# Small routing and choice work from GpSimd to VectorE, the last two diagonals to ScalarE, scatters and zero stores a step sooner, and row loads ahead of weight loads, in a recurrence, mixture and feed-forward kernel

## The chip, the cores and the metric

The kernel runs on one core of a Trainium2 chip. The metric is the device time of one execution in microseconds (us). TensorE (PE) multiplies matrices and writes PSUM; VectorE (DVE), ScalarE (ACT) and GpSimd (POOL) work element by element; SyncE (SP) issues most DMA transfers, GpSimd the indirect ones (scatters). Each engine carries out its own instructions in order, and waits at an instruction until what it needs is there.

## The reference

The computation has three parts. A recurrence over 768 time steps (batch 4, 8 heads, head size 48) gives 3072 rows of 384 numbers; a mixture of eight experts sends each row to the expert with the largest logit; a feed-forward part follows.

```python
for t in range(S):                       # S = 768, per batch and head
    cur = einsum('bhd,bhe->bhde', u[None] * kt, vt)
    y[:, :, t] = einsum('bhd,bhde->bhe', rt, state + cur)
    state = w[None, :, :, None] * state + einsum('bhd,bhe->bhde', kt, vt)
...
logits = x @ w_gate                      # x: 3072 x 384, 8 experts
expert_idx = argmax(logits, axis=1)
for e in range(E):
    h = maximum(xe @ w1[e], 0.0)         # 384 -> 1024
    out[mask] = gate_w[mask, None] * (h @ w2[e])   # 1024 -> 384
...
h = x @ w_in                             # 384 -> 2048
return maximum(0.01 * h, h) @ w_out      # 2048 -> 384
```

For the reference's inputs the eight experts get 410, 409, 403, 389, 380, 374, 359 and 348 rows.

## The kernel before

**Attention.** The recurrence is done in chunks: 24 units (`n`, 6 chunks of 128 tokens times 4 batches), and a loop of 25 steps that is software-pipelined by hand. In step `n` PE makes the scores of unit `n` (L490), the values of unit `n-1` (L520, L526), its state update (L511, for units under 20) and turns the values of unit `n-2` into rows (L565). DVE lays the masked scores over the diagonal (L496), scales K and R of unit `n+2` (L432) and sums `av` (L460). POOL makes `kr` (L451, for units under 20) and `rk` (L446, L447) of unit `n+3`. ACT writes the diagonal `A` of unit `n+1` as eight activations (L479); for units 22 and 23 POOL writes it as one product (L472). SP loads inputs ahead and, from step `ZERO_AT`, stores zeros over the spare rows of one expert region per step (L415).

**Routing.** Four units are a group. `ROUTE_AT` puts the four parts of a group's routing at fixed steps: part 0 the largest logit (L707 to L716), part 1 the one-hot choice `oh` (L718 to L726), part 2 the prefix counts on PE and the running count `carry` (L732 to L748), part 3 the row index `ix` (L751 to L755). On steps under 20 POOL does a part of it. `SCATTER_AT` puts the scatters (L759, issued by POOL) of each unit's 128 rows into the DRAM table `xs`, one region per expert. `choose_first` (steps 16 to 18) picks the expert that leads after three groups, and `early_flag` (steps 20, 21) tells whether that one has 256 rows after four.

**Experts.** The leading expert starts early, with a window of its first 256 rows, loaded by POOL as soon as the scatters of groups 0 to 3 have landed (L864, step 21); its other 224 follow as window 1, after all scatters. Windows 2 to 8 are the other experts, by size, with a fixed room each (`CAPS`). A window's rows are loaded as `w` partitions times `nj` rows (L861 to L866) into the one buffer `erows`, turned on PE (L880), split into two fp32r parts `xe` (ACT L883, DVE L884), and multiplied in eight steps (`first` L903, `second` L928). Beside it come the weights: one piece of 384 KB per step (L781, three `raw` buffers), of which ACT rounds the high part (L794) and DVE or POOL takes the low part (L802), and the conversion of 64-bit weights (load L812, ACT L822, DVE L832 to L852, store L854). The last part (L1022, L1041) is 414 us of PE work.

The order on each engine is the order of the code: nothing is reordered by a scheduler. On SP the row load of the next window stands behind the weight piece of the same step:

```python
if n + AHEAD >= nf:
    self.piece_load(n + AHEAD)
if n >= nf:
    if f == 0 and i + 1 < len(WINDOWS):
        self.load_rows(i + 1, xs)
```

Of the kernel before, what the change touches and what calls it, by code (L numbers as in the profile page):

```python
# [21 lines left out]
P = 128  # L22
NC = S // P
NU = NC * B
# [9 lines left out]

TB = 4

WARM = 5
ZERO_AT = 3

VO = 5  # L40

SCATTER_AT = {
    **{11 + 4 * g + u: [(g, u)] for g in (0, 1) for u in range(4)},
    19: [(2, 0), (2, 1)],
    20: [(2, 2), (2, 3)],
    21: [(3, u) for u in range(4)],
    24: [(4, u) for u in range(4)],
}

# [14 lines left out]
LISTS = 4  # L64
OUT_AT = (0, 1, 3, 5, 7, 9, 11, 13)

CAPS = (480, 456, 432, 416, 400, 392, 384, 372)
EARLY = 256
WINDOWS = [(0, 0, EARLY), (0, EARLY, CAPS[0] - EARLY)] + [(k, 0, CAPS[k]) for k in range(1, 8)]
PAD = 260  # L70
# [14 lines left out]
class Kernel:  # L85
# [149 lines left out]

    def choose_first(self, keep, part):

        V, G = self.nc.vector, self.nc.gpsimd
        if part == 0:
            f = lambda nm, w=1, dt=F32: keep.tile([1, w], dt, name=nm)  # L240
            _, self.half_key = self.counts(keep, "half", G)
            self.half_mx, self.half_x, self.half_id = f("half_mx"), f("half_x", E), f("half_id")
            self.lead, self.first_i = f("lead", E), f("first_i", 1, I32)
        elif part == 1:
            V.tensor_reduce(out=self.half_mx, in_=self.half_key, axis=AX.X, op=ALU.max)
            G.tensor_scalar(
                out=self.lead, in0=self.half_key, scalar1=self.half_mx, scalar2=None, op0=ALU.is_equal
            )
            G.tensor_tensor(out=self.half_x, in0=self.lead, in1=self.place, op=ALU.mult)
        else:  # L250
            V.tensor_reduce(out=self.half_id, in_=self.half_x, axis=AX.X, op=ALU.add)
            G.tensor_scalar(
                out=self.first_i, in0=self.half_id, scalar1=float(E - 1), scalar2=0.0, op0=ALU.min, op1=ALU.max
            )

# [8 lines left out]

    def early_flag(self, keep, part):

        V, G = self.nc.vector, self.nc.gpsimd
        if part == 0:
            self.early_cnt, _ = self.counts(keep, "early", G)
            G.tensor_tensor(out=self.early_cnt, in0=self.early_cnt, in1=self.lead, op=ALU.mult)  # L270
        else:
            self.redo = n = keep.tile([1, 1], F32, name="early_n")
            V.tensor_reduce(out=n, in_=self.early_cnt, axis=AX.X, op=ALU.add)
            V.tensor_scalar(out=n, in0=n, scalar1=float(EARLY), scalar2=None, op0=ALU.is_lt)
# [70 lines left out]
    def attention(self, xs, clist, extra, first_weights, const, route):  # L345
        nc, tc, a = self.nc, self.tc, self.a
        with ExitStack() as ctx:
# [27 lines left out]
            nc.sync.dma_start(out=u1, in_=a["u"])  # L375
            self.u_row = one.tile([P, DM], F32, name="u_row")
            load(0, ("k", "r", "kT", "rT"))
            load(1, ("kT", "rT", "k", "r"))
            load(0, ("v",))
            load(2, ("k", "r"))  # L380
            load(1, ("v",))
# [82 lines left out]
            def prep_diag(n):  # L464
                if n >= NU:
                    return
                d = st[n]
                d["A"] = wk.tile([P, 2, NP, P], F32, tag="A", name="A")
                if n >= NU - 2:

                    flat = d["A"].rearrange("s i p t -> s p i t")
                    nc.gpsimd.tensor_tensor(  # L472
                        out=flat, in0=self.ident[:, None, None, :].to_broadcast([P, NP, 2, P]),
                        in1=d["av"].rearrange("s (p i) -> s p i", i=2)[:, :, :, None].to_broadcast([P, NP, 2, P]),
                        op=ALU.mult,
                    )
                    return
                for h in range(H):
                    nc.scalar.activation(  # L479
                        out=d["A"][:, h % 2, h // 2, :], in_=self.ident, func=AF.Copy,  # L480
                        scale=d["av"][:, h : h + 1],
                    )
# [113 lines left out]
            for n in range(NU + 1):  # L596

                ahead = [n + 2] if n < 18 else [2 * n - 16, 2 * n - 15] if n < 20 else []
                for m in ahead:
                    load(m, ("kT", "rT"))  # L600
                for m in ahead:
                    load(m + 1, ("k", "r"))
                if n == 19:

                    first_weights()
                for m in ahead:
                    load(m, ("v",))
# [12 lines left out]
                if 0 <= n - 1 < NU:  # L620
                    values(n - 1)
                    update(n - 1)
                if 0 <= n - 2 < NU - 1:
                    rows(n - 2)

                rows_out(n - 3)
                if n - 2 >= B:
                    state(n - 2)

                if n < NU:  # L630
                    masked(n)
                if 0 < n <= B:
                    state(n - 1)
                prep_T(n + 2)
                if n:
                    prep_kr2(n + 1)
                prep_rk(n + 3)
                if 0 < n <= VO:
                    values_out(n - 1)
                if n + 1 < NU - 2:  # L640
                    prep_diag(n + 1)
                prep_av(n + 2)
                if n + 2 >= NU - 2:
                    prep_diag(n + 2)
                if VO <= n - 1 < NU:
                    values_out(n - 1)
                decay(n - 1)
                extra(n)
                if n == 3:
                    self.late_tables(one, route, const)  # L650
                elif n == 5:
                    self.later_tables(one, const)
                elif n == NU - 2:
                    self.safe_decays(one, const)
                    self.cap_table()
                for part, g in ROUTE_AT.get(n, ()):
                    bank = None
                    if part == 2:
                        bank = st[n - 1].get("bank") or update_bank(n - 1)
                        bank = bank[:, NP * D : NP * D + 5 * E]  # L660

                    self.route(part, g, route, nc.gpsimd if n < 20 else nc.vector, bank)
                if 16 <= n < 19:
                    self.choose_first(const, n - 16)
                elif 20 <= n < 22:
                    self.early_flag(const, n - 20)
                for g, u in SCATTER_AT.get(n, ()):
                    self.scatter(g, u, xs)
                if n == NU - 3:

                    self.load_rows(0, xs, nc.gpsimd)
# [24 lines left out]
    def route(self, part, g, sm, eng, bank=None):  # L696
# [20 lines left out]
        elif part == 1:  # L717
            nc.scalar.activation(out=d["ex"][:, :, 0:E], in_=d["df"], func=AF.Exp)  # L718
            d["m2"], d["oh"] = f("m2", [P, B]), f("oh16", [P, B, E], BF16)
            V.tensor_reduce(out=d["m2"], in_=d["eq"], axis=AX.X, op=ALU.max)  # L720
            if eng is V:
                V.tensor_tensor(out=d["oh"], in0=d["eq"], in1=be(d["m2"]), op=ALU.is_equal)
            else:
                eng.tensor_tensor(out=d["eq"], in0=d["eq"], in1=be(d["m2"]), op=ALU.subtract)
                eng.tensor_scalar(out=d["oh"], in0=d["eq"], scalar1=0.0, scalar2=None, op0=ALU.is_equal)
            eng.tensor_copy(  # L726
                out=d["rows"].bitcast(I32)[:, :, DM + 1], in_=self.tokid[:, B * g : B * (g + 1)]
            )
# [126 lines left out]
            del self.conv[i]  # L855


    def load_rows(self, i, xs, eng=None):

        k, off, cap = WINDOWS[i]  # L860
        nj = -(-cap // P)  # L861
        w = cap // nj
        self.win[i] = t = self.rowpool.tile([P, 4, RW], F32, tag="rows", name="erows")
        (eng or self.nc.sync).dma_start(  # L864
            out=t[:w, :nj, :],
            in_=xs[bass.ds(self.ids[k] * NT + off, cap), :].rearrange("(j p) c -> p j c", p=w),  # L866
        )

    def turn(self, i, ps, tag, cs=range(KD)):
        nc = self.nc  # L870
        k, off, cap = WINDOWS[i]
        nj = -(-cap // P)
        w = cap // nj
        for c in cs:
            if c == 0:
                self.xT[i] = self.xpool.tile([P, 2, KD, 512], F32R, tag="x", name="xe")
# [69 lines left out]
    def experts(self, xs, clist, pools, meanwhile):  # L946
# [10 lines left out]
                self.second(*next(rest), pools)  # L957

        for n, (i, f) in enumerate(seq):
            if n + AHEAD >= nf:  # L960
                self.piece_load(n + AHEAD)
            if n >= nf:
                if f == 0 and i + 1 < len(WINDOWS):
                    self.load_rows(i + 1, xs)
                if f == 6:
                    for k in {1: (1,), 2: (2, 3), 3: (4, 5), 4: (6, 7)}.get(i, ()):
# [341 lines left out]
def main_path(k, ctx, const, out, xs, clist, debug):  # L1308
# [8 lines left out]
            k.piece_load(i)  # L1317

    def extra(n):
        for i in {20: (0,), 21: (1,), 22: (2,), 23: (3, 4), 24: (5,)}.get(n, ()):  # L1320
            k.piece_high(i)
        for i in {21: (0,), 22: (1, 2), 23: (3, 4), 24: (5,)}.get(n, ()):
            k.piece_low(i)
        for i in {21: (3,), 22: (4, 5), 23: (6, 7)}.get(n, ()):
            k.piece_load(i)

    kw = dict(reuse_waits="tile")
# [92 lines left out]
```

## Time and profile before

| | us |
|---|---|
| median of 3 runs | 796.58 (795.02 to 797.38) |
| the profiled execution | 795.89 |
| its span | 794.2 |
| busy in the span: PE, DVE, ACT, POOL | 755.1, 471.9, 372.5, 198.3 |

The span is what the trace holds; 1.69 us of the profiled execution lie around it. All times of the rows count from the start of the span. [...]

### The profile page before, as it was taken

What the parts mean: (1) busy time and instruction counts of PE and PEld (TensorE: products, weight loads), DVE (VectorE), ACT (ScalarE), POOL (GpSimd) and SP (SyncE); (2) the same over time, 40 slices, a digit from 0 to 9 for tenths busy, and PEclk for the clock granted to TensorE, in tenths of its full rate; (3) what the DMA queues carried; (4) which work ended last, traced back from release to release, by engine and by line L of the source; (5) the groups of instructions that cost most, each with busy time, mean ns of one, the idle gap of its engine ahead of it and who ended that gap; (6) DMA issues with size and microseconds to landing.
All of it is one profiled execution on the core that took longest, in us unless ns stands there. A gap on an engine that the chain in (4) does not pass through costs nothing.

```text
span 794.2 us, 13196 instructions
## 1 busy us (share of the span) xinstructions
PE 755.1 (95%) x4908; PEld 694.2 (87%) x4908; DVE 471.9 (59%) x837; ACT 372.5 (47%) x785; POOL 198.3 (25%) x216
## 2 busy tenths in 40 slices
PE   6999995989999999799999999999999999999994
PEld 3889884989999999799999899999999999999993
DVE  6898885548888999699873443433333343343330
ACT  6898873355545555356443523332342243233331
POOL 6867885401222222122200110020020001002001
PEclk9999997899999999999999999999999999999997
DMA  8997965368767757757530000010010001001001
GB/s 250 264 272 225 281 223 179 121 184 257 210 193 230 232 183 232 204 162 228 147 111 21 6 35 1 1 40 0 1 40 1 1 0 40 1 1 40 1 1 44
DMA packets 52372, 92.62 MB, mean 117 GB/s; under 512 B 12788, under 2 KB 30761, under 8 KB 52297
## 3 DMA queue, kind: packets, MB, share of 16 engines
q1 hardware_dynamic: 49017, 81.47, 34.6%
q0 software_dynamic: 3280, 10.21, 3.5%
q8 instruction: 40, 0.66, 0.4%
q14 instruction: 35, 0.29, 0.1%
HBM read 73.11 MB, written 18.57 MB: 115 GB/s over the span
## 4 chain that ended last, share of the span: by engine, by line
PE 75%; DMA 9%; POOL 7%; issue 3%; DVE 2%; SPq 2%; ACT 0%; POOLq 0%; ACTq 0%
PE o L1041 25%; PE ph L1022 25%; PE ph L903 12%; PE y L928 11%; DMA r<-in_r 3%; DMA erows<-xs 3%; DMA xs<-z 2%; POOL rk L446 2%; POOL xs L759 2%; POOL rk L447 1%; PE pt L880 1%; DMA raw<-in_wE 1%; SPq L368 1%; POOL kr L451 1%; DMA xs<-rows,ix 1%
## 5 line engine op out<-in xcount | busy, mean ns | idle before, releaser
L1041 PE MATMUL o<-c,gg 128*128 128x384 f32 x1152 | 215.5, 336 | 0.0
L1022 PE MATMUL ph<-x,c 128*128 128x512 f32 x864 | 213.9, 392 | 0.0
L1041 PEld LDWEIGHTS o<-c,gg 128*128 128x128 f32 x1152 | 202.1, 188 | 8.1 <-DVE gg L1031 0.2
L1022 PEld LDWEIGHTS ph<-x,c 128*128 128x128 f32 x864 | 161.2, 188 | 28.5
L1028 DVE TENSOR_TENSOR s<-s,ph 128x512 f32<-128x512 f32 x96 | 65.9, 686 | 165.4 <-ACT s L1027 165.4
L1027 ACT ACTIVATE s<-ph 128x512 f32<-128x512 f32 x96 | 57.4, 598 | 173.9 <-PE ph L1022 162.7
L903 PE MATMUL ph<-xe,c 128*128 128x256 f32 (+8 forms) x648 | 124.8, 338 | 0.0
L928 PE MATMUL y<-hh,c 128*128 128x256 f32 (+8 forms) x648 | 122.4, 333 | 1.2 <-DVE hh L909 0.7
L802 POOL TENSOR_TENSOR c<-raw,c 128x768 fp32r<-128x768 f32 x32 | 60.2, 1880 | 223.3 <-ACT c L794 159.7
L928 PEld LDWEIGHTS y<-hh,c 128*128 128x128 f32 x648 | 110.2, 189 | 3.7 <-DVE hh L909 0.9
L903 PEld LDWEIGHTS ph<-xe,c 128*128 128x128 f32 x648 | 109.8, 192 | 1.9
L1031 DVE TENSOR_TENSOR gg<-s,gg 128x512 fp32r<-128x512 f32 x96 | 66.4, 692 | 67.0 <-ACT gg L1030 66.3
L1054 POOL DMA_INDIRECT out<-z,to x24 | 24.2, 1008 | 320.9 <-ACT z L1053 302.6
L1030 ACT ACTIVATE gg<-s 128x512 fp32r<-128x512 f32 x96 | 60.7, 632 | 81.2 <-DVE s L1028 81.2
L794 ACT ACTIVATE c<-raw 128x768 fp32r<-128x768 f32 x80 | 67.1, 840 | 6.7 <-DMA raw<-in_wE 5.9
L908 ACT ACTIVATE hh<-ph 128x256 fp32r<-128x256 f32 (+8 forms) x72 | 34.4, 478 | 68.5 <-PE ph L903 65.4
L802 DVE TENSOR_TENSOR c<-raw,c 128x768 fp32r<-128x768 f32 x48 | 46.0, 962 | 13.7 <-ACT c L794 12.0
L479 ACT ACTIVATE A<-ident,av 128x128 f32<-128x128 f32 x176 | 53.8, 396 | 0.5 <-DVE av L460 0.4
L849 DVE SCALAR_TENSOR_TENSOR t<-raw,t 128x384 f32<-128x384 uint32 x32 | 44.3, 1384 | 1.1
L909 DVE SCALAR_TENSOR_TENSOR hh<-ph,hh 128x256 fp32r<-128x256 f32 (+8 forms) x72 | 38.5, 535 | 6.1 <-ACT hh L908 5.9
L496 DVE COPY_PREDICATED A<-strict,pa 128x1024 f32<-128x1024 int32 x24 | 32.4, 1351 | 3.1 <-ACT A L479 1.2
L490 PE MATMUL pa<-R,K 48*128 48x128 f32 x384 | 28.2, 287 | 5.8 <-DVE A L496 5.8
(176 smaller groups left out, 681.1 us busy)
## 6 DMA issues: line engine op xcount, KB each, us to landing
raw<-in_wE SPq DMA_DIRECT2D x64, 384.0 KB
raw<-in_w2nd SPq DMA_DIRECT2D x32, 384.0 KB
w2f<-t SPq DMA_DIRECT2D x32, 192.0 KB
raw<-w2f SPq DMA_DIRECT2D x16, 384.0 KB
k<-in_k SPq DMA_DIRECT2D x24, 192.0 KB
r<-in_r SPq DMA_DIRECT2D x24, 192.0 KB
v<-in_v SPq DMA_DIRECT2D x24, 192.0 KB
kT<-in_kT SPq DMA_DIRECT2D x40, 96.0 KB
```

Source lines behind the costliest of these rows:

```text
L479: nc.scalar.activation(out=d["A"][:, h % 2, h // 2, :], in_=self.ident, func=AF.Copy, scale=d["av"][:, h : h + 1],)
L794: self.nc.scalar.activation(out=w[:, 0, c], in_=t, func=AF.Copy)
L802: eng.tensor_tensor(out=w[:, 1, c], in0=t, in1=w[:, 0, c].bitcast(F32), op=ALU.subtract)
L849: nc.vector.scalar_tensor_tensor(out=x, in0=low.bitcast(U32), scalar=2.0**-52, in1=x, op0=ALU.mult, op1=ALU.mult)
L903: nc.tensor.matmul(ph[:, :cap], w[:, wl, c * 512 + o : c * 512 + o + P], self.xT[i][:, xl, c, :cap], start=(c == 0 and n == 0), stop=(c == ...
L928: nc.tensor.matmul(self.y[i][m][:, :cap], w[:, wl, o : o + P], t[:, xl, :cap], start=(f == 0 and n == 0), stop=(f == FF // P - 1 and n == 2),)
L1022: nc.tensor.matmul(ph, w[:, wl, c * 512 + off : c * 512 + off + P], x2[b][:, xl, c, :], start=(c == 0 and i == 0), stop=(c == KD - 1 and i ...
L1027: nc.scalar.activation(out=s, in_=ph, func=AF.Copy, scale=0.01)
L1028: nc.vector.tensor_tensor(out=s, in0=s, in1=ph, op=ALU.max)
L1030: nc.scalar.activation(out=t[:, 0, :], in_=s, func=AF.Copy)
L1031: nc.vector.tensor_tensor(out=t[:, 1, :], in0=s, in1=t[:, 0, :].bitcast(F32), op=ALU.subtract)
L1041: nc.tensor.matmul(o[b][k][:, :DM], t[:, gl, k * P : (k + 1) * P], w[:, wl, (f % 4) * DM : (f % 4 + 1) * DM], start=(f == 0 and i == 0), s ...
```

## The change

The GpSimd half of part 1 of the routing goes to VectorE in every group, group 3's routing wholly, and `choose_first` and `early_flag` too. The diagonals of units 22 and 23 are written by ScalarE like the others. Scatters, zero stores and the empty list `no_tokens` come a step sooner; the first conversions of weights come a step later. Two warm-up matmuls are left out, and of unit 1 `k` and `r` are loaded before their turned forms. From window 2 on, the row load of the next window stands ahead of the weight piece. The rooms become multiples of 16 (456, 392 and 372 become 448, 400 and 368), and `window` takes the smallest `nj` that divides the room.

```diff
-WARM = 5
-ZERO_AT = 3
+WARM = 3
+ZERO_AT = 2
 SCATTER_AT = {
-    **{11 + 4 * g + u: [(g, u)] for g in (0, 1) for u in range(4)},
...
+    **{10 + 4 * g + u: [(g, u)] for g in (0, 1) for u in range(4)},
...
+    20: [(2, 3), (3, 0)],
+    21: [(3, u) for u in range(1, 4)],
...
-CAPS = (480, 456, 432, 416, 400, 392, 384, 372)
+CAPS = (480, 448, 432, 416, 400, 400, 384, 368)
...
-            _, self.half_key = self.counts(keep, "half", G)
+            _, self.half_key = self.counts(keep, "half")
...
-            G.tensor_tensor(out=self.half_x, in0=self.lead, in1=self.place, op=ALU.mult)
+            V.tensor_tensor(out=self.half_x, in0=self.lead, in1=self.place, op=ALU.mult)
...
-            self.early_cnt, _ = self.counts(keep, "early", G)
+            self.early_cnt, _ = self.counts(keep, "early")
...
-            load(1, ("kT", "rT", "k", "r"))
+            load(1, ("k", "r", "kT", "rT"))
...
-                if n >= NU - 2:
-
-                    flat = d["A"].rearrange("s i p t -> s p i t")
-                    nc.gpsimd.tensor_tensor(
...
-                if n + 1 < NU - 2:
-                    prep_diag(n + 1)
+                prep_diag(n + 1)
                 prep_av(n + 2)
-                if n + 2 >= NU - 2:
-                    prep_diag(n + 2)
...
-                    self.route(part, g, route, nc.gpsimd if n < 20 else nc.vector, bank)
+                    self.route(part, g, route, nc.gpsimd if n < 18 else nc.vector, bank)
...
-            if eng is V:
-                V.tensor_tensor(out=d["oh"], in0=d["eq"], in1=be(d["m2"]), op=ALU.is_equal)
-            else:
-                eng.tensor_tensor(out=d["eq"], in0=d["eq"], in1=be(d["m2"]), op=ALU.subtract)
-                eng.tensor_scalar(out=d["oh"], in0=d["eq"], scalar1=0.0, scalar2=None, op0=ALU.is_equal)
+            V.tensor_tensor(out=d["oh"], in0=d["eq"], in1=be(d["m2"]), op=ALU.is_equal)
...
+    def window(self, i):
+
+        k, off, cap = WINDOWS[i]
+        nj = next(n for n in range(-(-cap // P), 5) if cap % n == 0)
+        return k, off, cap, nj, cap // nj
...
         for n, (i, f) in enumerate(seq):
+
+            if i > 1 and f == 0 and i + 1 < len(WINDOWS):
+                self.load_rows(i + 1, xs)
             if n + AHEAD >= nf:
                 self.piece_load(n + AHEAD)
             if n >= nf:
-                if f == 0 and i + 1 < len(WINDOWS):
+                if i == 1 and f == 0:
                     self.load_rows(i + 1, xs)
...
-        for i in {20: (0,), 21: (1,), 22: (2,), 23: (3, 4), 24: (5,)}.get(n, ()):
+        for i in {21: (0,), 22: (1,), 23: (2, 3, 4), 24: (5,)}.get(n, ()):
             k.piece_high(i)
-        for i in {21: (0,), 22: (1, 2), 23: (3, 4), 24: (5,)}.get(n, ()):
+        for i in {22: (0, 1), 23: (2, 3, 4), 24: (5,)}.get(n, ()):
             k.piece_low(i)
-        for i in {21: (3,), 22: (4, 5), 23: (6, 7)}.get(n, ()):
+        for i in {22: (3, 4), 23: (5, 6, 7)}.get(n, ()):
             k.piece_load(i)
```

On POOL, in steps 19 to 21 of attention, before: `rk` is the product of step 19 and 20, `A` the diagonals, `early_*` the early flag, `DMA xs` the scatters, the last row the load of the first window.

```order
L446 TENSOR_TENSOR rk<-r,k 128x384
L447 TENSOR_TENSOR rk<-rk,u_row 128x384
L724 TENSOR_TENSOR eq<-eq,m_1890 128x32
L725 TENSOR_SCALAR oh_1891<-eq 128x32
...
L472 TENSOR_TENSOR A<-ident,av 128x4x2x128
L230 TENSOR_TENSOR early_cnt<-carry,region 1x8
...
L759 DMA xs<-rows,ix 24576x386 x2
L472 TENSOR_TENSOR A<-ident,av 128x4x2x128
L759 DMA xs<-rows,ix 24576x386 x4
L864 ISA
L864 DMA erows<-xs 128x2x386
```

The same place of the changed kernel (its line numbers are others):

```order
L448 TENSOR_TENSOR rk<-r,k 128x384
L449 TENSOR_TENSOR rk<-rk,u_row 128x384
L745 DMA xs<-rows,ix 24576x386 x2
L448 TENSOR_TENSOR rk<-r,k 128x384
L449 TENSOR_TENSOR rk<-rk,u_row 128x384
L745 DMA xs<-rows,ix 24576x386 x5
L854 ISA
L854 DMA erows<-xs 128x2x386
```

Only the products, the scatters and the load are left there; seven scatters stand in these steps instead of eight.

On ACT, the last steps of attention before: `rows` and `xT` are the outputs of the units, `c` the high parts of the weights, `xe` the turned rows of the first window.

```order
L535 ACTIVATE xT_145<-py 112x512
L545 ACTIVATE St_143<-St_143,pw 112x112 x4
L794 ACTIVATE c_1968<-raw 128x768
L577 ACTIVATE rows<-pr 128x384
L535 ACTIVATE xT_146<-py 112x512
...
L535 ACTIVATE xT_146<-py 112x512
L794 ACTIVATE c_2152<-raw 128x768
L883 ACTIVATE xe<-pt 128x256 x3
```

And of the changed kernel:

```order
L528 ACTIVATE xT_145<-py 112x512
L538 ACTIVATE St_143<-St_143,pw 112x112 x4
L570 ACTIVATE rows<-pr 128x384
L472 ACTIVATE A<-ident,av 128x128 x8
L528 ACTIVATE xT_146<-py 112x512
...
L528 ACTIVATE xT_146<-py 112x512
L780 ACTIVATE c_2156<-raw 128x768
L871 ACTIVATE xe<-pt 128x256 x3
```

The diagonal's eight activations stand in steps 21 and 22, the conversions start a step later, and the piece that precedes `xe` is still the sixth.

On SP, the load of the last window before (`raw<-in_wE` is a weight piece, `raw_4307` the 64-bit weights):

```order
L781 DMA raw<-in_wE 128x768
L781 ISA
L781 DMA raw<-in_wE 128x768
L864 ISA
L864 DMA erows<-xs 124x3x386
L812 DMA raw_4307<-in_w2nd 128x768
```

And of the changed kernel:

```order
L767 DMA raw<-in_wE 128x768
L854 ISA
L854 DMA erows<-xs 92x4x386
L767 ISA
L767 DMA raw<-in_wE 128x768
L798 DMA raw_4314<-in_w2nd 128x768
```

The row load stands one piece further ahead, and its shape is 92 partitions of four rows instead of 124 of three.

## Rows read from the trace of the kernel before

**Rows 1.** PE, end of attention: start, us, what, idle before it.
```profile
90.87 0.18 PE L732 MATMUL pu<-oh,tri 128*128 128x32 bf16 x1 [1.56 <-POOL oh L725]
...
139.53 1.54 PE L880 MATMUL pt<-ident,erows 128*128 128x128 f32 x6 [7.86 <-DMA erows<-xs]
...
142.43 2.85 PE L903 MATMUL ph<-xe,c 128*128 128x256 f32 x18
```

**Rows 2.** The chain that ended last: start, us, what.
```profile
130.17 5.16 DMA xs<-rows,ix
...
164.75 7.23 DMA raw<-in_wE
```

**Rows 3.** Stretches: us, busy PE, PEld, DVE, ACT, POOL, clock, DMA share, GB/s.
```profile
84.60:111.80 27.20, 25.25 (x338) 22.88 (x336) 22.10 (x48) 24.35 (x79) 23.53 (x39) 0.94 0.86 260
111.80:131.60 19.80, 17.84 (x189) 15.35 (x185) 15.97 (x41) 7.24 (x14) 17.30 (x16) 0.91 0.55 189
...
295.00:321.90 26.90, 26.90 (x156) 26.78 (x155) 26.06 (x40) 14.59 (x27) 7.39 (x5) 1.00 0.70 228
```

**Rows 4.** PE, windows 7 and 8.
```profile
318.33 0.49 PE L880 MATMUL pt<-ident,erows 128*128 128x128 f32 x3
...
336.72 0.88 PE L880 MATMUL pt<-ident,erows 124*128 124x124 f32 x3 [5.14 <-DMA erows<-xs]
337.26 3.23 PE L903 MATMUL ph<-xe,c 128*128 128x384 f32 x9
340.29 2.26 PE L928 MATMUL y<-hh,c 128*128 128x384 f32 x9
342.39 1.72 PE L903 MATMUL ph<-xe,c 128*128 128x384 f32 x9
```

**Rows 5.** SP's queue, windows 7 and 8.
```profile
317.67 4.77 SPq L781 DMA_DIRECT2D raw<-in_wE  x2
322.67 0.28 SPq L864 DMA_DIRECT2D erows<-xs  x1
```

**Rows 6.** POOL in order of time, steps 15 and 20 to 21 of attention.
```profile
90.20 0.23 POOL L724 TENSOR_TENSOR eq<-eq,m 128x32 f32<-128x32 f32 x1
...
90.77 0.18 POOL L726 COPY rows<-tokid 128x4 int32<-128x4 int32 x1
...
118.25 0.92 POOL L230 TENSOR_TENSOR early_cnt<-carry,region 1x8 f32<-1x8 f32 x1
...
120.31 1.06 POOL L759 DMA_INDIRECT xs<-rows,ix  x1 [0.38 <-issue]
121.68 2.52 POOL L759 DMA_INDIRECT xs<-rows,ix  x1 [0.30 <-DVE A L496]
124.22 1.91 POOL L472 TENSOR_TENSOR A<-ident,av 128x1024 f32<-128x1024 f32 x1
```

**Rows 7.** ACT, end of attention.
```profile
107.92 2.44 ACT L479 ACTIVATE A<-ident,av 128x128 f32<-128x128 f32 x8
...
132.20 0.84 ACT L794 ACTIVATE c<-raw 128x768 fp32r<-128x768 f32 x1
```

**Rows 8.** One us of the stretch after the last row load's wait.
```profile
338.00:339.00 1.00, 1.00 (x4) 1.00 (x4) 0.76 (x3) 0.89 (x3) 0.00 (x0) 0.50 0.26 101
```

**Rows 9.** ACT, window 7: a piece converted, and the wait behind it.
```profile
328.85 0.84 ACT L794 ACTIVATE c<-raw 128x768 fp32r<-128x768 f32 x1
337.59 0.55 ACT L822 ACTIVATE size<-raw 128x384 f32<-128x384 f32 x1 [7.89 <-DMA raw<-in_w2nd]
```

**Rows 10.** Matmul groups by shape: busy us, mean ns.
```profile
L928 PE MATMUL y<-hh,c 128*128 128x456 f32 x72 | 16.1, 368 | 0.0
...
L928 PE MATMUL y<-hh,c 128*128 128x372 f32 x72 | 13.3, 332 | 0.0
```

**Rows 11.** ACT near the start.
```profile
13.26 0.23 ACT L595 ACTIVATE idwg<-wg 112x32 f32<-112x32 f32 x1 [2.01 <-DMA wg<-in_wg]
```

**Rows 12.** POOL near the start, while zeros are stored.
```profile
42.40 1.01 POOL L446 TENSOR_TENSOR rk<-r,k 128x384 f32<-128x384 f32 x1 [2.06 <-DMA r<-in_r]
```

More of the change, by code (lines that the diff above doesn't have):

```diff
@@ L35 @@
 TB = 4
-WARM = 5
-ZERO_AT = 3
+WARM = 3
+ZERO_AT = 2
 VO = 5
 SCATTER_AT = {
-    **{11 + 4 * g + u: [(g, u)] for g in (0, 1) for u in range(4)},
-    19: [(2, 0), (2, 1)],
-    20: [(2, 2), (2, 3)],
-    21: [(3, u) for u in range(4)],
+    **{10 + 4 * g + u: [(g, u)] for g in (0, 1) for u in range(4)},
+    18: [(2, 0)],
+    19: [(2, 1), (2, 2)],
+    20: [(2, 3), (3, 0)],
+    21: [(3, u) for u in range(1, 4)],
     24: [(4, u) for u in range(4)],
@@ L236, in choose_first @@
     def choose_first(self, keep, part):
-        V, G = self.nc.vector, self.nc.gpsimd
+        V = self.nc.vector
         if part == 0:
             f = lambda nm, w=1, dt=F32: keep.tile([1, w], dt, name=nm)
-            _, self.half_key = self.counts(keep, "half", G)
+            _, self.half_key = self.counts(keep, "half")
             self.half_mx, self.half_x, self.half_id = f("half_mx"), f("half_x", E), f("half_id")
@@ L245, in choose_first @@
             V.tensor_reduce(out=self.half_mx, in_=self.half_key, axis=AX.X, op=ALU.max)
-            G.tensor_scalar(
+            V.tensor_scalar(
                 out=self.lead, in0=self.half_key, scalar1=self.half_mx, scalar2=None, op0=ALU.is_equal
             )
-            G.tensor_tensor(out=self.half_x, in0=self.lead, in1=self.place, op=ALU.mult)
+            V.tensor_tensor(out=self.half_x, in0=self.lead, in1=self.place, op=ALU.mult)
         else:
             V.tensor_reduce(out=self.half_id, in_=self.half_x, axis=AX.X, op=ALU.add)
-            G.tensor_scalar(
+            V.tensor_scalar(
                 out=self.first_i, in0=self.half_id, scalar1=float(E - 1), scalar2=0.0, op0=ALU.min, op1=ALU.max
@@ L265, in early_flag @@
     def early_flag(self, keep, part):
-        V, G = self.nc.vector, self.nc.gpsimd
+        V = self.nc.vector
         if part == 0:
-            self.early_cnt, _ = self.counts(keep, "early", G)
-            G.tensor_tensor(out=self.early_cnt, in0=self.early_cnt, in1=self.lead, op=ALU.mult)
+            self.early_cnt, _ = self.counts(keep, "early")
+            V.tensor_tensor(out=self.early_cnt, in0=self.early_cnt, in1=self.lead, op=ALU.mult)
         else:
@@ L468, in prep_diag @@
                 d["A"] = wk.tile([P, 2, NP, P], F32, tag="A", name="A")
-                if n >= NU - 2:
-                    flat = d["A"].rearrange("s i p t -> s p i t")
-                    nc.gpsimd.tensor_tensor(
[L473 to L477, printed above, removed]
                 for h in range(H):
@@ L855, in convert @@
             del self.conv[i]
+    def window(self, i):
+        k, off, cap = WINDOWS[i]
+        nj = next(n for n in range(-(-cap // P), 5) if cap % n == 0)
+        return k, off, cap, nj, cap // nj
     def load_rows(self, i, xs, eng=None):
-        k, off, cap = WINDOWS[i]
-        nj = -(-cap // P)
-        w = cap // nj
+        k, off, cap, nj, w = self.window(i)
         self.win[i] = t = self.rowpool.tile([P, 4, RW], F32, tag="rows", name="erows")
@@ L870, in turn @@
         nc = self.nc
-        k, off, cap = WINDOWS[i]
-        nj = -(-cap // P)
-        w = cap // nj
+        k, off, cap, nj, w = self.window(i)
         for c in cs:
```

## The prediction

> **What bounds the kernel now.** I read four views in this order. First PE in order of time, with the idle time before each instruction, since PE is busy for 755 of 794 us: what can be won is what PE waits for, or does slowly. In the end of attention PE waits 1.56 us for the one-hot choice that POOL makes, and 7.86 us for the first window's rows, which it turns at 139.53; the first expert matmuls start at 142.43 [rows 1]. Then the chain that ended last: its step before those rows is a scatter issued at 130.17 that takes 5.16 us [rows 2]. From that scatter's start to PE's turn it is 139.53 − 130.17 = 9.36 us, so the first window hangs on when POOL issues its last early scatter. Third the stretches: between 84.6 and 131.6 PE idles 27.20 − 25.25 + 19.80 − 17.84 = 3.9 us, and the clock's means of 0.94 and 0.91 cost about 0.06 × 27.2 + 0.09 × 19.8 = 3.4 us, while POOL is busy for 23.53 of 27.2 and 17.30 of 19.8 us [rows 3]. In the windows later PE has no idle time (26.90 of 26.90), with one exception: the last window's rows come 5.14 us late, and the clock that is at half behind that wait makes the next step slow [rows 4]. SP says why they come late: the row load stands behind two weight pieces, the second of which waits for a buffer, and is issued at 322.67 only [rows 5].
>
> **Routing, choice and diagonals (the start of the first window).** POOL stops doing the following from step 15 on. Fourteen small products and copies of the choice in steps 15 to 19; two instructions there lie 90.77 − 90.20 = 0.57 us apart, so 0.285 us each, 4.0 us. Two diagonals at 1.91 us, 3.8 us. The early flag, from 118.25 to the scatter at 120.31, 2.1 us. One scatter that now stands before these steps: 121.68 − 120.31 = 1.4 us. Together 11.3 us [rows 6]. The scatter at 121.68 took 2.52 us and the one before it 1.06 [rows 6]; if that excess of 1.5 us goes too, it is 12.8. POOL was the late one over this whole stretch [rows 3], so the last early scatter comes at about 130.17 − 11.3 = 118.9, and with the same 9.36 us behind it the rows are there at 128.2. PE itself ends attention at 131.6 now and gets back at most 3.9 + 3.4 = 7.3 us: 124.3, which is sooner than the rows, so a wait of some 4 us stays and it is still the rows that are late.
>
> The moved work lands on engines that have less room than POOL. ACT takes two diagonals of 2.44 us [rows 7] and is at 24.35 of 27.2 us in the first of the stretches, 15.97 of 19.8 us for DVE in the second, and only 7.24 of 19.8 us for ACT there [rows 3], which is where the diagonals go. Conversions of weights, one of them at 132.20 [rows 7], stand ahead of `xe` on ACT and a step later than before. That one, the sixth, comes just behind PE's end of attention at 131.6; with PE's 7.3 us back it would be at 124.9, and as its load now starts a step later, I put it up to 2 us later, at 127: close under the rows' 128.2 but not over. I take −11.0: POOL's 11.3 less a little for these. Bounds: −13 (with the scatter's excess), and −4 where PE's own pace, held by ACT, DVE and a DMA share that is 0.86 at 260 GB/s already [rows 3], is what remains.
>
> **Row loads ahead of weight pieces.** Before, the last row load was issued at 322.67 and its rows were used at 336.72, 14.0 us later [rows 4, 5]. Now it waits only for its buffer, which PE's last turn of window 7 frees at 318.33 + 0.49 = 318.8 [rows 4]; with 0.28 us for the issue, 319.1, that is 3.6 us sooner. 368 rows are 1% fewer bytes than 372, so by the nearest row it takes 14.0 us again and lands at 333.1, while PE is ready at 336.72 − 5.14 = 331.6: a wait of 1.5 us instead of 5.1. But something else is late next. The piece that was issued before it, at 317.67 + 4.77 − 0.34 = 322.1 [rows 5], and converted at 328.85 [rows 9], now stands behind it in the queue. The 64-bit weights that stood behind it before landed 337.59 − 336.72 = 0.9 us after the rows [rows 4, 9]; with the piece and these weights both behind, I put the piece at 334.0 and the weights at 334.9. ACT does the piece, these weights and then `hh` in that order; the second-layer matmuls stood 340.29 − 337.59 = 2.7 us behind the weights [rows 4, 9], so they start at about 337.6, and with 9 × 0.172 = 1.6 us for them at the full clock [rows 3] the step that began at 342.39 starts at 339.2: −3.2, taken as −3.0 as the clock will not be whole at once. Bounds: the whole loss, 342.39 − 331.6 less the turn's 0.25 and one step of 18 matmuls at 0.172 us (26.9 / 156), so −7.4; and −2 if the clock drops for as long as before.
>
> The trace shows that the DMA engines were busy for a share of 0.26 at 101 GB/s just after this wait, as if 4 of 16 worked [rows 8]. [...] No run here shows yet what 92 partitions do.
>
> **The rest.** The room of 456 rows is 114 partitions of four, that of 448 is 112. The chain passes a weight piece that took 7.23 us [rows 2] at that window, where one in window 7 was converted 328.85 − 322.44 = 6.4 us after its issue [rows 5, 9]: at most −0.8, at least 0, taken as −0.6. The rooms' widths change by −8, +8 and −4 columns in 144 matmuls each; a column costs (368 − 332) / 84 = 0.43 ns [rows 10], so −4 × 144 × 0.43 ns = −0.25, with bounds of −0.3 and 0. The two warm-up matmuls and the order of unit 1's loads cost nothing: what PE's first diagonals wait for begins with ACT at 13.26, which waits for the gate weights from DMA, and that load is not changed [rows 11]. Zero stores a step sooner meet the loads at the start; POOL already waits 2.06 us for `r` there [rows 12], and the stores take their share one step longer beside it: between 0 and +1.3, taken as +0.5.
>
> Sum: −11.0 − 3.0 − 0.6 − 0.25 + 0.5 = −14.35. The profiled execution took 795.89 us (span 794.2 and 1.69 around it), so 781.5; it lies 0.7 under the median of the three runs.
>
> **Rivals.**
> (1) All of it comes back: the last load spreads over more engines, the scatter's excess goes, zeros cost nothing. −13 − 7.4 − 0.8 − 0.3 = −21.5, 774.4 us. [...]
> (2) POOL was not alone late: PE, ACT and DVE with loads near the limit keep the start's gain at half. −5.5 in place of −11: 787.0. ACT's 24.35 of 27.2 us speaks for it [rows 3]; POOL's sum, and the wait on its choice [rows 1], against it.
> (3) The change does not do what it says at the start: the sixth conversion, or the window's rows behind the denser scatters, holds the first `ph` where it was, and only the later terms are left: −3.35, 792.5.
> (4) Slower: weight pieces that now stand behind a row load are late in each of six windows. ACT converts in order, and a late piece holds back `hh`, as the late 64-bit weights did for 7.89 us [rows 9]. It decides when a piece lands over 6.4 + 3.1 = 9.5 us after its issue, a step later than it is converted now; then some 4 us (half that wait) are lost per window: +24 on 781.5, 805.5 us. Against it: before the last window the loads in the stretch from 295 make no wait at all, with a DMA share of 0.70 [rows 3].
>
> **How the numbers follow.** My forecast (777 to 785) 0.54, rival 1 0.13, rival 2 0.20, rival 3 0.08, rival 4 0.05. The range of 773 to 789 holds the forecast, rival 1 and rival 2, and leaves out 3 and 4, 0.13, and some tails. About 0.3% is what a measurement of this kernel can tell from no change: faster 0.94, the same 0.01, slower 0.05.
>
> **What would show it.** The wait of PE on the one-hot choice is gone; the last scatter before the first row load is issued near 119, the first turn starts at 127 to 129, the first expert `ph` near 131. The last row load is issued near 319, its turn waits about 1.5 us, and a second wait, on `hh`, stands close behind. If the first `ph` starts after 137, or a window's steps wait for pieces, the forecast is wrong; if the last load takes under 9 us, the row behind 14.0 was the wrong one.

## The result and the profile after

The changed kernel took 784.85 us (median of 3 runs, 782.67 to 784.85) beside 796.58 before: a ratio of 0.9847, with a 95% interval of 0.9812 to 0.9881. The forecast was 781.5, in a range of 773 to 789. Timed again on a chip with other kernels it took 788.99 (785.53 to 790.84) beside 797.68, a ratio of 0.9883 [0.9863, 0.9904]; that is at the upper end of the range. The profiled execution has a span of 783.2 us, 11.0 less than the 794.2 before.

Where the 11.0 us come from is read by laying PE's rows of both traces side by side at fixed points of the program. First the start of the experts: PE after the change, in the columns of [rows 1].

```profile
26.75 1.16 PE L483 MATMUL pa<-R,K 48*128 48x128 f32 x16
...
122.34 1.16 PE L483 MATMUL pa<-R,K 48*128 48x128 f32 x16
...
130.97 0.18 PE L718 MATMUL pu<-oh,tri 128*128 128x32 bf16 x1 [0.83 <-DVE oh L711]
...
131.17 0.85 PE L868 MATMUL pt<-ident,erows 128*128 128x128 f32 x6
...
135.76 3.90 PE L891 MATMUL ph<-xe,c 128*128 128x256 f32 x18 [2.47 <-DVE xe L872]
...
156.88 1.38 PE L868 MATMUL pt<-ident,erows 112*128 112x112 f32 x6 [3.06 <-DMA erows<-xs]
...
160.01 4.61 PE L891 MATMUL ph<-xe,c 128*128 128x224 f32 x27
164.46 1.17 PE L916 MATMUL y<-hh,c 128*128 128x224 f32 x9
...
171.50 0.55 PE L868 MATMUL pt<-ident,erows 112*128 112x112 f32 x4
```

The same points of the kernel before that were not shown yet: the scores `pa` of units 3 and 23, the turn of window 1's rows and what follows it.

```profile
24.95 1.16 PE L490 MATMUL pa<-R,K 48*128 48x128 f32 x16
...
121.67 1.16 PE L490 MATMUL pa<-R,K 48*128 48x128 f32 x16 [1.26 <-DVE A L496]
...
161.69 0.80 PE L880 MATMUL pt<-ident,erows 112*128 112x112 f32 x6 [1.88 <-DMA erows<-xs]
...
163.41 3.17 PE L903 MATMUL ph<-xe,c 128*128 128x224 f32 x27
166.41 1.17 PE L928 MATMUL y<-hh,c 128*128 128x224 f32 x9
...
175.19 0.55 PE L880 MATMUL pt<-ident,erows 114*128 114x114 f32 x4
```

Subtract. Unit 3 starts 1.8 us later than before, unit 23 still 0.7 later: between them PE took 95.6 us for 96.7. The 7.86 us of waiting for the first rows [rows 1] are gone, so the first turn is 8.4 us sooner; the first `ph` is 6.7 sooner, since it now waits 2.47 us for `xe`; behind window 1's turn only 164.46 − 166.41 = −1.95 us are left. Of the 4.7 us lost in between, 2.9 lie behind the start of that turn, where the clock is at half (0.51 between 156 and 163; the 27 matmuls take 4.61 for 3.17 us). The other 1.9 lie before it, mostly as the first 18 matmuls take 3.90 for 2.85 us, and as the turn waits 3.06 for 1.88. At the first turn of window 2 it is −3.7. From there the difference stays: the third turn of window 7 stands at 314.57, −3.76 against 318.33 [rows 4]. The last window gives the rest:

```profile
314.57 0.49 PE L868 MATMUL pt<-ident,erows 128*128 128x128 f32 x3
...
327.76 0.48 PE L868 MATMUL pt<-ident,erows 92*128 92x92 f32 x4
328.02 1.83 PE L891 MATMUL ph<-xe,c 128*128 128x384 f32 x9
...
334.43 0.48 PE L868 MATMUL pt<-ident,erows 92*128 92x92 f32 x4
```

No wait at all, where there were 5.14 us and a slow step [rows 4]. The second turn of the last rows stood at 345.53 before; 334.43 is −11.1, so this window is worth −7.3. SP's queue shows why: the row load goes out at 315.09, right behind the last turn of window 7, and the piece behind it at 318.32.

```profile
315.09 0.29 SPq L854 DMA_DIRECT2D erows<-xs  x1
318.32 0.35 SPq L767 DMA_DIRECT2D raw<-in_wE  x1
```

The stretches of [rows 3], after the change, and two us in which the last row load was almost alone on the queues (columns as there; the last three are clock, DMA share and GB/s). The stretches are fixed times, and the changed kernel gets through more matmuls in them:

```profile
84.60:111.80 27.20, 25.05 (x360) 22.13 (x356) 26.15 (x59) 23.51 (x77) 23.60 (x28) 1.00 0.90 266
...
111.80:131.60 19.80, 18.06 (x212) 15.69 (x207) 16.14 (x49) 14.94 (x41) 7.70 (x8) 1.00 0.67 220
...
317.00:319.00 2.00, 2.00 (x13) 2.00 (x12) 1.97 (x2) 1.42 (x3) 1.30 (x1) 1.00 0.25 80
```

POOL is busy for 7.7 us in the second stretch, where it was 17.30; DVE went from 22.10 to 26.15 of 27.2 us in the first. PE's idle time there is 27.20 − 25.05 = 2.15 us, where it was 1.95; its clock is at 1.00 in both stretches. What PE waits for in the first one is DVE: the one-hot choice `oh`, which POOL made before, takes 2.40 us there, and the state update `St` that PE needs stands behind it.

```profile
88.29 2.40 DVE L711 TENSOR_TENSOR oh<-eq,m 128x32 bf16<-128x32 f32 x1
```
```profile
91.57 0.57 PE L504 MATMUL pu<-v,kr 128*48 128x48 f32 x16 [1.48 <-DVE St L549]
```

So the wait of 1.56 us for POOL's `oh` [rows 1] is gone, and 1.48 us behind DVE's `oh` stand in its place. The rest of PE's idle time in this stretch is two shorter waits for `St`.

### The profile page after: what moved, and what is told of

Read it like the earlier page. It is cut to its first block, busy times and chain, and to the rows that moved or that the text cites. A ratio compares the mean times of both kernels' runs of the same rounds, so it can differ in the third digit from the quotient of the medians.

```text
span 783.2 us, 13206 instructions
## 1 busy us (share of the span) xinstructions
PE 753.3 (96%) x4907; PEld 694.0 (89%) x4907; DVE 475.2 (61%) x854; ACT 377.8 (48%) x801; POOL 186.6 (24%) x192
## 4 chain that ended last, share of the span: by engine, by line
PE 78%; DMA 1%; issue 1%; POOL 0%; ACT 0%; POOLq 0%
PE o L1032 25%; PE ph L1013 25%; PE y L916 13%; PE ph L891 13%; PE pt L868 1%; DMA erows<-xs 1%; POOL xs L745 0%; POOL out L1045 0%; ACT z L1044 0%; PE ok L222 0%; POOLq L1091 0%; POOLq L854 0%; POOLq L1045 0%
## 5 line engine op out<-in xcount | busy, mean ns | idle before, releaser
L891 PE MATMUL ph<-xe,c 128*128 128x400 f32 (+7 forms) x648 | 125.8, 341 | 2.5 <-DVE xe L872 2.5
L916 PE MATMUL y<-hh,c 128*128 128x400 f32 (+7 forms) x648 | 122.4, 334 | 0.0
L896 ACT ACTIVATE hh<-ph 128x400 fp32r<-128x400 f32 (+7 forms) x72 | 34.4, 478 | 71.9 <-PE ph L891 70.4
L472 ACT ACTIVATE A<-ident,av 128x128 f32<-128x128 f32 x192 | 58.5, 391 | 0.3 <-DVE av L462 0.2
L897 DVE SCALAR_TENSOR_TENSOR hh<-ph,hh 128x400 fp32r<-128x400 f32 (+7 forms) x72 | 38.5, 535 | 9.2 <-ACT hh L896 9.2
```

The source lines that it names most:

```text
L472: nc.scalar.activation(out=d["A"][:, h % 2, h // 2, :], in_=self.ident, func=AF.Copy, scale=d["av"][:, h : h + 1],)
L891: nc.tensor.matmul(ph[:, :cap], w[:, wl, c * 512 + o : c * 512 + o + P], self.xT[i][:, xl, c, :cap], start=(c == 0 and n == 0), stop=(c == ...
L916: nc.tensor.matmul(self.y[i][m][:, :cap], w[:, wl, o : o + P], t[:, xl, :cap], start=(f == 0 and n == 0), stop=(f == FF // P - 1 and n == 2),)
```

## The experiments

**The engine moves, undone.** Choice, leader, early flag and the last two diagonals back on GpSimd; scatter steps, rooms and row loads as changed.

```diff
-            self.early_cnt, _ = self.counts(keep, "early")
+            self.early_cnt, _ = self.counts(keep, "early", self.nc.gpsimd)
...
-                    self.route(part, g, route, nc.gpsimd if n < 18 else nc.vector, bank)
+                    self.route(part, g, route, nc.gpsimd if n < 20 else nc.vector, bank)
...
+                if n >= NU - 2:
+                    nc.gpsimd.tensor_tensor(out=flat, ...)
+                    return
```

> The changed kernel with all the engine moves undone (choice, leader and early flag on GpSimd, the last two diagonals too); the earlier scatters, rooms and row loads stay. Theory (the moves freed GpSimd by some 10 us but the first window then waits for the end of attention on PE, DVE and ACT): the last early scatter comes 8 to 11 us later again, near 128 to 130; the first turn waits for its rows; the first ph starts near 141, plus 4 to 6 us, 789 to 791. Rival (the earlier scatters did it): the last early scatter stays before 123 and the time within 1.5 us of the changed kernel's.

Measured: 792.23 us, ratio 0.9919 [0.9887, 0.9951]. Of the kernels timed with it that keep the moves, the two that also keep rooms and row loads have 0.9817 and 0.9827 (each has one edit of its own, below), the one with the old rooms 0.9883; the changed kernel itself has 0.9847 and 0.9883 in its two timings. By these medians the moves are worth 3 to 8 us; at the low end the intervals overlap. The last early scatter on POOL, and PE:

```profile
131.64 0.97 POOL L761 DMA_INDIRECT xs<-rows,ix  x1 [0.31 <-issue]
```
```profile
141.20 1.54 PE L884 MATMUL pt<-ident,erows 128*128 128x128 f32 x6 [5.81 <-DMA erows<-xs]
...
144.10 3.88 PE L907 MATMUL ph<-xe,c 128*128 128x256 f32 x18
```

With the moves that scatter stands at 119.74 and the row load, on POOL too, at 123.61:

```profile
119.74 0.97 POOL L745 DMA_INDIRECT xs<-rows,ix  x1 [0.30 <-issue]
123.61 0.79 POOL L854 DMA_DIRECT2D erows<-xs  x1 [2.89 <-DMA xs<-rows,ix]
```

The scatter stands 11.9 us later here and the first `ph` 8.3, but attention itself stood 3.35 us later in this profile (unit 23's scores at 125.69). Counted from the start of unit 23's scores, in us:

| | last early scatter | first `ph` |
|---|---|---|
| before | +8.50 | 20.76 |
| moves undone | +5.95 | 18.41 |
| after the change | −2.60 | 13.42 |

So in these profiles the moves bring the scatter 8.55 us forward, remove the wait for the rows, and give the first `ph` 5.0 us. The rest of the change, the earlier scatters among it, gives 2.55 and 2.35 us. In the eleven profiles that keep the moves (all but the one with late zeros) the scatter stands between −2.6 and −3.6. The moves did not quicken attention: from unit 16's scores to unit 23's it takes 35.8 us with the moves undone, 35.5 after the change, and 35.1 to 40.3 in the eleven; 37.0 before.

**The sixth piece, converted later.** What the first `ph` waits for now is read on DVE (the low halves of `c`, the turned rows `xe`), and ahead of it on ACT, both after the change:

```profile
132.86 0.96 DVE L788 TENSOR_TENSOR c<-raw,c 128x768 fp32r<-128x768 f32 x1 [1.77 <-ACT c L780]
...
134.63 1.07 DVE L872 TENSOR_TENSOR xe<-pt,xe 128x256 fp32r<-128x256 f32 x3
```
```profile
131.98 0.85 ACT L780 ACTIVATE c<-raw 128x768 fp32r<-128x768 f32 x1
132.72 0.93 ACT L871 ACTIVATE xe<-pt 128x256 fp32r<-128x256 f32 x3
```

```diff
-        for i in {21: (0,), 22: (1,), 23: (2, 3, 4), 24: (5,)}.get(n, ()):
+        for i in {21: (0,), 22: (1,), 23: (2, 3, 4), }.get(n, ()):
...
-        if n in (1, 2):
+        if n in (0, 1, 2):
             k.piece_split(n + 5)
```

> The changed kernel with the sixth piece's two halves converted after the first ph instead of before the first xe. Theory (the first ph waits 2.47 us for xe, which stands behind that conversion on ACT and DVE): the wait falls by 1 to 2 us and the first ph starts about 4 instead of 4.6 us behind the first turn's start or less; time 1 to 2 us lower. Rival (xe is held by the PSUM turn and the route work behind it alone): nothing, or the later conversion holds hh back and the time rises by up to 1 us.

Measured: 783.02 us, ratio 0.9817 [0.9794, 0.9839]. The first turn and `ph` of PE:

```profile
132.83 1.41 PE L868 MATMUL pt<-ident,erows 128*128 128x128 f32 x6
...
135.59 2.74 PE L891 MATMUL ph<-xe,c 128*128 128x256 f32 x18
```

From turn to `ph` it is 2.76 us instead of 4.59, and no wait: that conversion alone cost 1.8 us in front of the first expert matmul. The times by themselves do not tell this kernel from the changed one (0.9847 [0.9812, 0.9881]).

**The row loads, behind the pieces again**, with the rooms as changed.

```diff
-            if i > 1 and f == 0 and i + 1 < len(WINDOWS):
-                self.load_rows(i + 1, xs)
...
-                if i == 1 and f == 0:
+                if f == 0 and i + 1 < len(WINDOWS):
                     self.load_rows(i + 1, xs)
```

> The changed kernel with each row load behind the weight piece of its step again; rooms stay as changed (last load 92 x 4). Theory: the place in SP's queue is the whole of the last window's gain; the last load is issued some 3.6 us later, PE waits about 4 to 5 us for it and the clock falls to half behind: plus 6 to 7.4 us, 791 to 792. Rival (the form 92 x 4 made the load quicker): the wait is under 2 us and the time rises by less than 3 us.

Measured: 789.35 us, ratio 0.9887 [0.9851, 0.9923]. PE at the last window:

```profile
317.47 0.49 PE L868 MATMUL pt<-ident,erows 128*128 128x128 f32 x3
...
333.61 0.88 PE L868 MATMUL pt<-ident,erows 92*128 92x92 f32 x4 [2.79 <-DMA erows<-xs]
334.20 3.23 PE L891 MATMUL ph<-xe,c 128*128 128x384 f32 x9
...
343.08 0.48 PE L868 MATMUL pt<-ident,erows 92*128 92x92 f32 x4
```

From the third turn of window 7 to the second turn of the last rows it is 25.61 us; 27.20 before, 19.86 after. So the place in the queue is worth 5.75 of 7.34 us. The wait is 2.79 and not 4 to 5: in this place the 92 x 4 load was used 11.8 us after its issue (321.81 to 333.61), the 124 x 3 load 14.0 [rows 4, 5]. Neither expectation holds whole.

**The old rooms, with the row loads ahead.**

```diff
-CAPS = (480, 448, 432, 416, 400, 400, 384, 368)
+CAPS = (480, 456, 432, 416, 400, 392, 384, 372)
...
-        nj = next(n for n in range(-(-cap // P), 5) if cap % n == 0)
+        nj = -(-cap // P)
```

> The changed kernel with the old rooms (456, 392 and 372 in place of 448, 400 and 368) and the old split of a room, so that the last load is 124 x 3 again; row loads stay ahead of the pieces. Theory: the place in the queue is what counts; the load is issued 3.6 us sooner than in the kernel before, takes 12 to 14 us, and PE waits for it at most 1.5 us: 785 to 787. Rival (the form 92 x 4 is what made the load quick, 11.7 us in place of 14.0 at the same place in the queue): a wait of 1.5 to 2 us and the half clock behind it, plus 3 us or more, 788.

Measured: 787.07 us, ratio 0.9883 [0.9861, 0.9905]. PE's first turn of the last rows, whose load was issued at 312.23:

```profile
326.44 0.54 PE L868 MATMUL pt<-ident,erows 124*128 124x124 f32 x3 [1.48 <-DMA erows<-xs]
326.74 1.81 PE L891 MATMUL ph<-xe,c 128*128 128x384 f32 x9
...
333.12 0.48 PE L868 MATMUL pt<-ident,erows 124*128 124x124 f32 x3
```

14.2 us again, a wait of 1.48, and the step behind it at full speed (clock 1.00 from 326 to 328). From the third turn of window 7 (311.71) to 333.12 it is 21.41 us, so the form of the load is worth the other 1.55. The total time is more above its neighbours than these 1.55 us. This trace cannot account for the rest: it is of the fastest of the four executions, 785.04. The scatter of attention's end (below) is of that size.

**The start: warm-up, load order, zeros.** One edit each: `WARM = 5`; `load(1, ("kT", "rT", "k", "r"))`; `ZERO_AT = 3`.

> The changed kernel with five warm-up matmuls again instead of three. Theory: PE's idle gap of 1.3 us before the first scores (9.4 to 10.7) and the waits behind it took the clock from 1.00 to 0.50 until 26 us; with the gap filled the clock holds through the first scores, unit 3's scores start near 25.0 instead of 26.75, and the whole gains about 1.8 us (784.85 to 783.0). Rival: the order of unit 1's loads makes the start late; then unit 3's scores stay between 26.5 and 27 and the time at 784.8.

> The changed kernel with kT and rT of unit 1 loaded before k and r again. Theory of the warm-up: nothing moves, unit 3's scores at 26.5 to 27, time within 0.5 us of 784.85. Rival (the loads' order costs): unit 3's scores 1.5 to 2 us sooner, time near 783.

> The changed kernel with the zero stores from step 3 again. Theory: the stores cost nothing of note, unit 15's scores within 0.5 us of 82.2 once the start is taken off, time within 0.5 us of 784.85. Rival (a step sooner the stores stand in the way of loads): the scores of units 4 to 15 come 0.5 to 1.3 us sooner.

Measured: 786.19 us (ratio 0.9839 [0.979, 0.9889]), 784.08 (0.9817 [0.977, 0.9864]) and 785.07 (0.9848 [0.9808, 0.9888]); unit 3's scores at 26.94, 25.80 and 26.36. The warm-up theory falls: with five matmuls PE has no gap before its first scores, and unit 3 is as late as with three. The clock between 16 and 20 us, after the change and with the old order of loads:

```profile
16.00:20.00 4.00, 2.32 (x32) 2.13 (x28) 1.43 (x3) 2.83 (x8) 3.84 (x5) 0.50 1.07 292
```
```profile
16.00:20.00 4.00, 3.37 (x40) 2.95 (x38) 1.85 (x3) 1.55 (x4) 3.84 (x5) 1.00 1.05 295
```

With warm-up and load order both as before:

```diff
-WARM = 3
+WARM = 5
...
-            load(1, ("k", "r", "kT", "rT"))
+            load(1, ("kT", "rT", "k", "r"))
```

> The changed kernel with the start of the kernel before: five warm-up matmuls and kT and rT of unit 1 first. Theory (the loads' order makes the second scores late and the clock falls; the warm-up alone did nothing): the clock holds at 1.00 from 12 to 20, unit 3's scores at 25.0 to 25.8, 1 to 1.8 us sooner, and the time 0 to 1.8 us lower than the control. Rival (later waits for inputs eat what the start gains): unit 3 is sooner but unit 23 is not, and the time is the control's within 0.5 us.

> The changed kernel itself, as a control for the two others timed beside it: 783 to 786; the scores of unit 3 between 25.6 and 27.4, those of unit 23 between 122 and 126, with the clock at half for some part of 12 to 26 us.

Measured: 787.5 us (0.9852 [0.9833, 0.9871]) against 788.99 (0.9883 [0.9863, 0.9904]) of the control: 1.5 us lower, with intervals that overlap. But in its profile unit 3 starts at 27.82, later than in the control (27.09), and the clock is 0.69 between 16 and 20. So the start is not settled. The control shows how wide the kernel's own scatter is: the same code as after, with unit 23's scores at 128.34 instead of 122.34 and its first `ph` at 141.65 instead of 135.76. The 6.0 us arise between units 17 and 19, which start at 92.81 and 109.73 in the control, and at 93.32 and 103.34 in the profile after the change:

```profile
94.78 2.40 DVE L232 TENSOR_TENSOR half_cnt<-carry,region 1x8 f32<-1x8 f32 x1
...
98.28 0.70 DVE L549 TENSOR_TENSOR St<-St,pu 48x192 f32<-48x192 f32 x2
```
```profile
99.12 0.88 PE L504 MATMUL pu<-v,kr 128*48 128x48 f32 x16 [3.08 <-POOL pos L734]
...
141.65 3.08 PE L891 MATMUL ph<-xe,c 128*128 128x256 f32 x18 [2.48 <-DVE xe L872]
```
```profile
99.00:108.50 9.50, 9.38 (x81) 8.54 (x81) 8.25 (x22) 7.23 (x24) 8.57 (x9) 0.50 0.89 272
```

Here it is the leader's count, moved from POOL to DVE too, that takes 2.40 us (0.28 after the change). PE's next matmuls start when DVE's `St` behind it is done (the releaser that the row names was done 0.7 us sooner), after a wait of 3.08 us, and the clock is at half for the 9.5 us behind. The kernel with the old start has the same: 2.42 us for that count, a wait of 2.60, unit 23 at 127.62. In each of the eleven profiles `oh` or this count takes 1.1 to 2.6 us in place of 0.2 to 0.3, and ends 0.02 to 0.07 us behind the end of a product on POOL. Why they take so long is not shown; no run moves these two alone.

**Zeros: fewer, and later.** 160 spare rows per region in place of 224 (`SURE = 320`), and the stores in steps 9 to 16 (`ZERO_AT = 9`).

> The changed kernel with zeros stored over 160 spare rows per region instead of 224 (2.7 MB become 1.9 MB). Theory (the inputs' arrival holds attention: DMA share 0.8 to 0.93 at 223 to 281 GB/s, GpSimd waits for r): 0.77 MB less is up to 3 us at 260 GB/s, unit 23's scores 1 to 3 us sooner than in the runs of the changed kernel (122 to 126) and the time 1 to 3 us lower. Rival (the engines hold it): nothing moves, 784 to 786.

> The changed kernel with the zero stores (2.7 MB) in steps 9 to 16 instead of 2 to 9. Theory (attention is held by the arrival of kT and r while the DMA share is near 0.9): units 12 to 18 take 5 to 10 us more than 29 to 34 us, and DVE's waits for kT grow from 1.4 to 3.6 us to over 5. Rival (the engines hold attention, DMA has room): units 12 to 18 stay within 29 to 35 us and units 3 to 12 take 40.3 us as before.

Fewer zeros: 783.18 us (0.9827 [0.9811, 0.9844]); unit 23's scores at 123.09, within the 122.3 to 128.4 of the others: no sign of a gain from these bytes at the start. Later zeros: 803.08 in one run. Units 12 to 18 took 109.60 − 66.49 = 43.1 us instead of 31.6 after the change (67.01 to 98.56), and units 3 to 12 40.5 instead of 40.3. What DVE and POOL wait for between 64 and 102 us (engine, instruction, releaser: us, times, longest), in this kernel and then after the change:

```profile
DVE K L434 <- DMA kT<-in_kT: 12.8, 4, 4.6
...
POOL xs L745 <- DMA xs<-z: 6.7, 4, 2.3
POOL rk L448 <- DMA r<-in_r: 4.9, 3, 1.8
```
```profile
DVE K L434 <- DMA kT<-in_kT: 2.6, 3, 1.8
```

So what is added to the queues in steps 9 to 16 delays `kT`. The scatters also waited for the zeros themselves, so not all of the 43.1 us is traffic. It is one profile, and it says nothing of the end of attention after the change: there the three waits for `kT` end at 82.30, and from 84.6 to 111.8 DVE waits for no input, and POOL 0.7 us for `r`.

**Old start and later piece together.**

> The old start and the sixth piece converted after the first ph, together. If both terms add: 2 to 3.5 us under the control. If only the piece counts: 1.5 to 2 us under it. If neither: within 0.5 us.

Measured: 782.01 us (778.83 to 784.7), ratio 0.9795 [0.9772, 0.9818], below the control's whole interval on the same chip: 7.0 us between the medians, twice the most that was expected. It is the fastest version here; its profile has the first `ph` at 135.32. The piece is worth the 1.8 us shown above; the rest is not split further, and the scatter of attention is part of it (unit 23's scores at 124.42, 3.9 us sooner than in the control).

## Why the prediction came out as it did

The range held the time and the likeliest case was near, but that is in part luck, as terms were off in opposite directions: up to the end of window 1 −1.95 came where −11.0 was forecast (with the start, and +0.5 for zeros), and −7.34 where −3.0 was forecast for the last window. By the forecast's own sign, a first `ph` after 137, the profile of the control (141.65) would have spoken against it.

*The first window, −11.0 forecast.* The step on POOL was right: the last early scatter was forecast at 118.9 and stands at 119.74. The step that failed is the next, that PE would get back 3.9 us of idle time and 3.4 us of clock, end attention at 124.3, and find the rows late. Both were put down to POOL. They were not POOL's: unit 23's scores start at 122.34 against 121.67, and between 122.3 and 128.4 in the eleven profiles that keep the moves. PE's idle time in the two stretches is 2.15 + 1.74 = 3.9 us, as before. The clock was whole after the change, but in the first stretch it is 0.81 to 1.00 in the eleven, and 1.00 with the moves undone. The wait went with the work: where PE had waited for the choice on POOL it waited behind the choice on DVE, which is busy for 26.15 of 27.2 us there. So this was the mechanism of rival 2, at a gain of −6.7 in this profile, with DVE and not ACT near its limit. The first turn then waited for nothing but the choice on DVE (0.83 us), and the conversion that I had put "close under" the rows, at 127, stood at 131.98 and cost 1.8 us.

*The start, "cost nothing".* Unit 3 stands 1.8 us later in the profile, and 0.7 to 2.5 us later in the nine profiles with this warm-up and this order of loads. No run separates what of it is scatter.

*Window 1, not priced.* I let the gain of the first window go through. Its rows depend on the last scatters, behind attention's end; PE reached the turn sooner and waited 3.06 us, with the clock at half behind it (0.51 between 156 and 163). Of 6.7 us 1.95 were left. That PE came sooner is not all of it: with the moves undone PE reaches this turn later than before (165.33 against 161.69), and still waits 3.18 us with a slow step behind (27 matmuls in 4.55 us). What else in the change does this is not shown.

*Window 2, −0.6 with a bound of −0.8.* From 166.41 to 175.19 it was 8.78 us, from 164.46 to 171.50 it is 7.04: −1.7. The wait behind the weight piece is gone wholly; my bound was too tight. And it is not the room: in every other kernel run here this stretch takes 7.03 or 7.04 us, the one with the old rooms (114 partitions) among them. Which edit removes the wait is not shown.

*The last window, −3.0 with a bound of −7.4.* It gave −7.3. The mechanism and the issue time were right (0.52 us behind PE's third turn of window 7 instead of 4.34, so 3.8 us sooner where I had 3.6). What failed is "by the nearest row it takes 14.0 us again": the 92 x 4 load is quicker by some 2 us than the 124 x 3 one, in two places of the queue (11.8 against 14.0; no wait against 1.48). With the old form the wait is 1.48 us where 1.5 was forecast. The second wait that I expected on ACT came, but cost PE nothing, as `hh` was made in time:

```profile
327.08 0.85 ACT L780 ACTIVATE c<-raw 128x768 fp32r<-128x768 f32 x1 [1.76 <-DMA raw<-in_wE]
```

Why the load is quicker is not shown. It does not show as a wider spread: between 317 and 319 us the load was almost alone, with a DMA share of 0.25, the time of four of the sixteen engines, and the 124 x 3 load of the old rooms, issued at 312.23, has 0.27 between 314 and 316:

```profile
314.00:316.00 2.00, 2.00 (x13) 2.00 (x13) 1.97 (x2) 1.51 (x3) 1.45 (x1) 1.00 0.27 90
```

[rows 8], from which I had read the four engines, does not show this load: its rows were in use from 336.72, before that stretch. In the traces' packets of 1544 bytes, one row each, a packet took 121 and 117 ns in the two 124 x 3 loads (before, and with the old rooms) and 102 and 90 ns in the 92 x 4 loads (behind the pieces, and after the change); on average about four were under way at once, before (372 × 121 ns in 11.3 us) and after the change (368 × 90 ns in 8.5). So the gain that rival 1 had for this window came, but the spread that it named does not show.

*Widths and zeros* (−0.25, +0.5): neither shows. From window 2 to window 7 the difference moves by 0.07 us, and zeros a step later gave the time of the changed kernel. *Rival 4* did not come: one piece was 1.76 us late on ACT, and no window waits for pieces.

In the trace the sum is −1.95 − 1.74 − 0.07 − 7.34 = −11.1, against −11.0 between the spans.

## What to carry to other kernels

When work is taken off an engine that is late, ask what the next engine will wait for then, and read it from a trace in which that engine is not late, or price the wait with the old time. Here the choice that held PE for 1.56 us on GpSimd held it for 1.48 us on VectorE, and the last matmuls of the choice at attention's end came only 0.3 us sooner (130.97 against 131.31). The last early scatter came 10.4 us sooner, the first expert matmul 6.7, and 2 us were left behind window 1. A transfer that must be early goes ahead of transfers whose issue waits for a buffer; two moved lines gave 5.75 of the 11 us here. Work in program order ahead of the first instruction of a new stage, such as a conversion that is needed later, is part of that stage's start: 1.8 us here.

## What was not expected of the hardware

Row loads of nearly equal bytes took 14.0 and 14.2 us from issue to use with 124 partitions of three rows (before, and with the old rooms), and 11.8 us with 92 partitions of four (behind the pieces). Where such a load was almost alone, the DMA share was nearly the same: 0.27 with the old rooms, 0.25 after the change. This was not pursued further. After a wait of 1.48 us, with the old rooms, PE's clock stayed at 1.00; after 2.79 us, behind the pieces, and 3.06 us, after the change, the following matmuls ran partly at half (clock 0.50 from 333 to 339, and 0.51 from 156 to 163); after 1.88 us, at window 1's turn, both were seen (27 matmuls in 3.17 us before, in 4.63 with the old rooms). A comparison of 128 x 32 numbers on VectorE took 2.40 us at 88.29 and 0.19 at 109.80 in one profile. And executions of one kernel differ by up to 6 us at the end of attention (first `ph` at 135.76 and 141.65), where one such slow instruction on VectorE stood before a wait of 3.08 us on PE and 9.5 us at the half clock.
